# The order of the loads of k and q, and of the casts of V, k and q, in a fused attention + SwiGLU kernel

## The chip, the cores and the metric

The kernel runs on one core of a Trainium2 chip. The metric is the device time of one execution in microseconds (us). "Span" is the time from the first to the last instruction in a profile, some 1.7 to 2.2 us less than the device time.

The engines: TensorE (PE in the profile, PEld its weight loads), VectorE (DVE), ScalarE (ACT), GpSimd (POOL), and SyncE (SP), which only issues DMA here.

## The reference

Causal attention with an additive bias made from a running sum of `s`, then a SwiGLU feed-forward on the result. Batch 8, 8 heads, 576 positions, head size 64; 4608 tokens, model 512, feed-forward 1536.

```python
scores = scale * np.matmul(q, k.transpose(0, 1, 3, 2))
cum = np.cumsum(np.maximum(s, 0.0), axis=-1)
bias = -(cum[:, :, :, None] - cum[:, :, None, :])
scores = np.where(causal, -1e9, scores + np.minimum(bias, 0.0))
attn = softmax(scores)                       # shortened
x = np.matmul(attn, v)                       # then to [4608, 512]
g = x @ w_gate
out = (g / (1 + exp(-g)) * (x @ w_val)) @ w_out
```

## The kernel before

Heads are counted through all batches, 0 to 63. A **half-batch** is four heads; it is the unit in which k and q are loaded (576 KB each), cast to bf16, transposed and used. V is loaded by batch (8 heads), in five chunks. "k 5" below means k of half-batch 5, "V 1" means V of batch 1.

Batch 0's attention runs alone. After that the attention of batch b+1 is woven into nine feed-forward stages of 512 tokens each, of which the first begins at about 30 us. All loads of k, q and V go through one queue, SyncE's, in program order. GpSimd does most of the casts, the causal masks, and issues weights and stores. A **mask** here is the step that blanks the scores of later positions; attention x V of a head cannot start before it.

```python
raw = ctx.enter_context(tc.tile_pool(name="raw", bufs=3))   # k, q as loaded: three half-batches
# ... V as loaded has one buffer (bufs=1): V b+1 waits until V b is cast
NPE = 5          # half-batches 0 to 4 are transposed on TensorE, later ones by DMA

def load_qk(hb):                       # on SyncE's queue
    load_one(hb, "k")
    load_one(hb, "q")

def prep_one(hb, i):                   # a quarter of a half-batch: transpose, copy to KQ
    g, nm = divmod(i, 2)
    nm = ("k", "q")[nm]
    pe_transpose(hb, nm, g)
    for r in range(2):
        pe_out(hb, nm, g, r, nc.scalar if nm == "k" else nc.vector)

PREP_AT = {      # at half-batch h, after (head in it, piece of its scores): which quarter of h + 1
    2: {(1, 3): 0, (2, 1): 1, (2, 3): 2, (3, 1): 3},
    3: {(0, 3): 0, (1, 3): 1, (2, 1): 2, (2, 3): 3},
}

def side(h, step):
    bh = HB * h + step
    if bh == H + 3:                                  # head 11: casts of V 1
        for c in range(5):
            cast_v(1, c, nc.gpsimd)
    if h >= 3 and h + 3 < NHB and step == 0:         # head 12: k, q 6, and so on
        load_qk(h + 3)
    # ... DMA transposes, casts, loads and casts of later V

def attn_items():
    for kk in range(H, BH + 2):
        h, step = divmod(kk, HB)
        if kk < BH:
            if step == 3 and h + 2 < NPE:            # head 11: casts of half-batch 4
                cast_one(h + 2, "k", nc.gpsimd)
                cast_one(h + 2, "q", nc.gpsimd)
            for ci in range(4):
                score_piece(kk, ci)
                if ci == 1:
                    side(h, step)
                # ... then prep_one where PREP_AT says so
        # ... attention x V of earlier heads

# in first_batch(), after the scores of head h:
                if h == 3:
                    aug(2, SP4)                      # bias rows, small DMAs
                    load_qk(3)
                if h == 7:
                    aug(3, SP4)
                    load_v(1, range(5))
                    load_qk(4)
                    cast_one(2, "k", nc.gpsimd)
                    cast_one(2, "q", nc.gpsimd)
                    w_load("o", 0)
                    w_load("o", 1)

hook = {         # after the n-th step of the first feed-forward stage
    # ... 1 to 4: the quarters of half-batch 2
    9: [lambda: cast_one(3, "k", nc.gpsimd), lambda: cast_one(3, "q", nc.gpsimd)],
    21: [lambda: load_qk(5)],
}
```

In the feed-forward, line 571 is the gate matmul, 586 the value matmul, 599 the output matmul. Line 367 is the scores, 405 attention x V, 291 the transposes of k and q, 388 and 383 the masks, 249 the casts of k and q, 176 those of V, 320 the copies of transposed q.

The softmax here doesn't subtract the row's maximum and nothing guards it: scores larger than these inputs give would overflow.

## Time and profile before

| | before |
|---|---|
| device time | 401.94 us median of 3 (400.12 to 403.02) |
| span of the profiled run | 401.8 us (device time 403.55) |
| TensorE busy | 373.3 us (93%) |
| first feed-forward stage | 32.07 to 94.70 us: 62.63 us |
| second, third stage | 42.79 and 40.25 us |

Stage lengths are from the first gate matmul of a stage to that of the next. The view of busy time by window has, for each stretch, its length, busy time (and instructions) of PE, PEld, DVE, ACT and POOL, the granted TensorE clock, the DMA engines' busy share and GB/s. The kernel before:

```profile
52.00:60.00 8.00, 5.45 (x27) 2.54 (x27) 4.75 (x8) 3.27 (x9) 2.96 (x4) 0.79 0.62 180
...
73.90:81.00 7.10, 0.43 (x13) 0.30 (x10) 0.76 (x3) 0.00 (x0) 2.60 (x5) 0.86 0.52 196
81.00:94.70 13.70, 13.38 (x110) 7.66 (x113) 2.87 (x8) 7.09 (x15) 10.72 (x19) 0.83 0.96 220
94.70:137.70 43.00, 42.46 (x373) 24.23 (x380) 30.35 (x57) 26.45 (x55) 27.50 (x46) 1.00 0.73 189
```

TensorE is busy only 5.45 of 8 us in 52 to 60, and in 73.9 to 81 us every engine is idle most of the time; and where TensorE works again its clock is low for some us. Such a stretch in which TensorE has nothing to do is called a **hole** below. The last line is the stage after (and 0.2 us of the next), for comparison: 42.46 of 43.00 us busy, clock 1.00.

### The profile page before, as it was taken

The page shows a single profiled execution, that of the slowest core. Times are in us where ns is not written, and L with a number is a line of the kernel's source. Part 1 is how long each engine was busy: PE and PEld are TensorE (multiplying, and loading weights), DVE is VectorE, ACT ScalarE, POOL GpSimd, SP SyncE. Part 2 cuts the span into 40 slices and gives each one's busy share as a digit, 9 for nine tenths or more (in the row PEclk, how much of TensorE's full clock was granted, in tenths as well). Part 3 has the DMA queues.
Part 4 walks back from the last instruction along what each step waited for, and adds up shares of the span by engine and source line. Part 5 has one row for each costly group of instructions (what it writes and reads, how often), then busy time and mean ns, then how long its engine had stood idle before and what let it go on. Part 6 is the DMA issues. An engine that isn't in the chain of part 4 may idle for free.

```text
span 401.8 us, 7873 instructions
## 1 busy us (share of the span) xinstructions
PE 373.3 (93%) x2943; PEld 207.3 (52%) x2994; DVE 241.5 (60%) x431; ACT 214.3 (53%) x411; POOL 192.4 (48%) x329
## 2 busy tenths in 40 slices
PE   4789979399999999999999999999999999999996
PEld 3575535255555555555555555555555554444442
DVE  7766756315885578627962795479627743842850
ACT  8576954245765665556555655565556522323321
POOL 7581436176578675667565756575542211001001
PEclk9999989979999999999999999999999999999999
DMA  7999975689685998899389939793531114002002
GB/s 248 223 268 207 197 185 125 234 213 244 153 185 148 278 288 176 204 286 232 106 197 277 232 112 190 217 208 104 97 127 27 23 25 135 2 22 82 2 0 105
DMA packets 100534, 64.18 MB, mean 160 GB/s; under 512 B 81888, under 2 KB 85824, under 8 KB 100496
## 3 DMA queue, kind: packets, MB, share of 16 engines
q1 hardware_dynamic: 90672, 45.23, 47.2%
q0 software_dynamic: 9680, 18.32, 17.1%
q8 instruction: 23, 0.38, 0.4%
q14 instruction: 15, 0.12, 0.1%
q10 hardware_dynamic: 144, 0.13, 0.1%
HBM read 37.90 MB, written 19.86 MB: 144 GB/s over the span
## 4 chain that ended last, share of the span: by engine, by line
PE 72%; DMA 9%; SPq 8%; issue 4%; DVE 2%; POOL 2%; ACT 2%; POOLq 0%; DVEq 0%; ACTq 0%
PE bank L599 20%; PE bank L571 18%; PE bank L586 18%; PE bank L367 8%; SPq L169 7%; PE bank L405 5%; DMA rawq<-in_q_dram 3%; DMA rawk<-in_k_dram 2%; DMA pk<-ks 2%; PE wide L367 2%; ACT pt L380 1%; SPq L152 1%; POOL vt L176 1%; DMA XT<-xs 1%; DMA kq<-HL 1%
## 5 line engine op out<-in xcount | busy, mean ns | idle before, releaser
L380 ACT ACTIVATE pt<-bank 128x512 bf16<-128x512 f32 x224 | 104.3, 504 | 52.4 <-PE bank L367 40.2
L578 DVE SCALAR_TENSOR_TENSOR pp<-th,bank 128x512 bf16<-128x512 bf16 x108 | 74.1, 686 | 74.5 <-ACT th L576 73.9
L571 PE MATMUL bank<-XT,wg 128*128 128x512 bf16 x409 | 110.5, 381 | 2.2 <-DMA XT<-xs 0.6
L586 PE MATMUL bank<-XT,wv 128*128 128x512 bf16 x421 | 110.0, 381 | 0.3
L576 ACT ACTIVATE th<-bank 128x512 bf16<-128x512 f32 x108 | 64.5, 597 | 79.3 <-PE bank L571 75.4
L599 PE MATMUL bank<-wo,ht 128*128 128x512 bf16 x415 | 103.5, 383 | 1.0 <-issue 0.2
L591 DVE TENSOR_TENSOR ht<-pp,bank 128x512 bf16<-128x512 bf16 x108 | 74.0, 685 | 9.8 <-PE bank L586 0.9
L367 PE MATMUL bank<-kq 128*128 128x128 bf16 (+4 forms) x504 | 66.7, 242 | 2.4 <-DVE kq L320 2.1
L367 PEld LDWEIGHTS <-kq 128*128 128x128 bf16 x576 | 47.3, 101 | 42.0 <-issue 6.5
L383 POOL TENSOR_SCALAR_AFFINE_SELECT pt<-pt 128x512 bf16<-128x512 bf16 x64 | 41.2, 644 | 43.4 <-ACT pt L380 42.8
L571 PEld LDWEIGHTS <-wg 128*128 128x128 bf16 x432 | 38.5, 98 | 36.9 <-issue 1.8
L599 PEld LDWEIGHTS <-ht 128*128 128x128 bf16 x432 | 38.7, 99 | 36.4 <-issue 1.1
L586 PEld LDWEIGHTS <-wv 128*128 128x128 bf16 x432 | 38.5, 98 | 35.5 <-issue 1.6
L405 PEld LDWEIGHTS <-pt 128*128 128x128 bf16 x960 | 41.8, 98 | 28.9 <-POOL pt L388 6.8
L405 PE MATMUL bank<-vt,pt 128*128 128x65 bf16 x840 | 43.3, 194 | 8.3 <-POOL pt L388 6.7
L439 POOL DMA_DIRECT2D xs<-ot x24 | 21.8, 910 | 58.9 <-DVE ot L422 58.9
L622 POOL DMA_DIRECT2D out_dram<-ysb x35 | 19.6, 562 | 60.9 <-ACT ysb L616 60.9
L616 ACT ACTIVATE ysb<-bank 128x512 f32<-128x512 f32 x35 | 20.9, 598 | 41.5 <-PE bank L599 38.5
L421 DVE RECIPROCAL rc<-bank 128x5 f32<-128x5 f32 x56 | 10.6, 190 | 40.0 <-PE bank L405 39.9
L190 POOL DMA_DIRECT2D kq<-HL x52 | 31.2, 602 | 2.3 <-PE bank L571 1.6
L422 DVE TENSOR_TENSOR ot<-bank,rc 128x320 bf16<-128x320 f32 x56 | 27.5, 492 | 1.9
L249 POOL CAST ck<-rawk 128x1152 bf16<-128x1152 f32 x14 | 16.1, 1148 | 19.3 <-DMA rawk<-in_k_dram 19.3
(66 smaller groups left out, 209.5 us busy)
## 6 DMA issues: line engine op xcount, KB each, us to landing
out_dram<-ysb POOLq DMA_DIRECT2D x35, 256.0 KB, 3.2
rawk<-in_k_dram SPq DMA_DIRECT2D x15, 576.0 KB, 4.8
rawq<-in_q_dram SPq DMA_DIRECT2D x15, 576.0 KB, 6.2
rawv<-in_v_dram SPq DMA_DIRECT2D x32, 256.0 KB, 4.6
xs<-ot POOLq DMA_DIRECT2D x24, 160.0 KB, 3.8
ks<-ck SPq DMA_DIRECT2D x11, 288.0 KB
qs<-cq SPq DMA_DIRECT2D x11, 288.0 KB, 3.9
wg<-in_moe_w_gate_dram POOLq DMA_DIRECT2D x2, 768.0 KB, 12.6
```

Source lines behind the costliest of these rows:

```text
L169: nc.sync.dma_start(t[0:n, c, :, :], v[b, :, c * 128 : c * 128 + n, :].rearrange("h p d -> p h d"),)
L190: engs[hh].dma_start(KQ[hb % 2][r][r0 : r0 + 4, :, e * S : (e + 1) * S], HL[bh : bh + 1, :, :, :],)
L367: nc.tensor.matmul(sc[:, o : o + w], T[:, 1, e * S + 128 * tj : e * S + 128 * (tj + 1)], T[:, 0, e * S + lo : e * S + hi], start=True, sto ...
L380: nc.scalar.activation(pt[:, c0 : c0 + W], sc[:, 0:W], AF.Exp, scale=0.125)
L383: nc.gpsimd.affine_select(pt[:, 1088:1600], pt[:, 1088:1600], pattern=[[0, 4], [1, 128]], compare_op=ALU.is_ge, fill=zreg, base=0, channel ...
L405: nc.tensor.matmul(av[:, bi * (D + 1) : (bi + 1) * (D + 1)], pt[:, c0 : c0 + 128], VT[b % 2][:, tj, h, :], start=(tj == 0), stop=(tj == bi),)
L571: nc.tensor.matmul(pg, WG[j][:, c, f0 : f0 + 128], xt[:, c, :], start=(c == 0), stop=(c == 3),)
L576: nc.scalar.activation(th, pg, AF.Tanh, scale=0.5)
L578: nc.vector.scalar_tensor_tensor(pp, in0=th, scalar=1.0, in1=pg, op0=ALU.add, op1=ALU.mult)
L586: nc.tensor.matmul(pv, WV[j][:, c, f0 : f0 + 128], xt[:, c, :], start=(c == 0), stop=(c == 3),)
L591: nc.vector.tensor_mul(ht, pp, pv)
L599: nc.tensor.matmul(py, hts[ft][:, ts_ * 128 : (ts_ + 1) * 128], WO[ft // WKO][:, ft % WKO, :], start=(ft == 0), stop=(ft == NFT - 1),)
```

## The change

The intent: the loads that are wanted first come first in SyncE's queue, and GpSimd does not stand at a cast whose data is still on its way while V 1 or masks are waiting behind it. `PREP_AT` also moves: half-batch 3 is prepared one head earlier, half-batch 4 one head later. No instruction is added or taken away.

```diff
         PREP_AT = {
-            2: {(1, 3): 0, (2, 1): 1, (2, 3): 2, (3, 1): 3},
-            3: {(0, 3): 0, (1, 3): 1, (2, 1): 2, (2, 3): 3},
+            2: {(0, 3): 0, (1, 3): 1, (2, 1): 2, (2, 3): 3},
+            3: {(1, 3): 0, (2, 1): 1, (2, 3): 2, (3, 1): 3},
         }
@@
-                    if step == 3 and h + 2 < NPE:
-                        cast_one(h + 2, "k", nc.gpsimd)
-                        cast_one(h + 2, "q", nc.gpsimd)
+                    if step == 1 and 3 < h + 1 < NPE:
+                        cast_one(h + 1, "k", nc.gpsimd)
+                        cast_one(h + 1, "q", nc.gpsimd)
@@
                 if h == 3:
                     aug(2, SP4)
-                    load_qk(3)
                 if h == 7:
                     aug(3, SP4)
+                    load_qk(3)
                     load_v(1, range(5))
                     load_qk(4)
                     cast_one(2, "k", nc.gpsimd)
                     cast_one(2, "q", nc.gpsimd)
+                    load_qk(5)
                     w_load("o", 0)
                     w_load("o", 1)
@@
-            9: [lambda: cast_one(3, "k", nc.gpsimd), lambda: cast_one(3, "q", nc.gpsimd)],
-            21: [lambda: load_qk(5)],
+            6: [lambda: cast_one(3, "k", nc.gpsimd), lambda: cast_one(3, "q", nc.gpsimd)],
```

## The prediction

> **What bounds the kernel now.** I read the page first, its 40 slices above all. Each slice is 10.05 us, a digit is tenths busy.
>
> ```profile
> PE   4789979399999999999999999999999999999996
> ...
> PEclk9999989979999999999999999999999999999999
> ```
>
> From slice 9 to slice 38 TensorE is full, so the kernel is TensorE-bound from about 90 us on. The holes are in slice 5 (50 to 60 us), slice 7 (70 to 80 us) and the low clock in slices 5 and 8. That is the first feed-forward stage, interleaved with the attention of batch 1. Its length comes from the windows: it runs from about 30 to 94.7 us.
>
> The view of TensorE in order of time shows the two holes, with what ended them:
>
> ```profile
> 54.21 0.38 PE L367 MATMUL bank<-kq 128*128 128x128 bf16 x4 [2.11 <-DVE kq L320]
> ...
> 80.90 0.35 PE L405 MATMUL bank<-vt,pt 128*128 128x65 bf16 x3 [6.67 <-POOL pt L388]
> ```
>
> The first: scores of head 12 (half-batch 3) wait for the last copy of its transposed q. The second: head 13's attention x V waits for a mask on GpSimd. GpSimd in order of time says why that mask was late:
>
> ```profile
> 56.78 1.15 POOL L249 CAST ck<-rawk 128x1152 bf16<-128x1152 f32 x1 [7.56 <-DMA rawk<-in_k_dram]
> 58.18 1.15 POOL L249 CAST cq<-rawq 128x1152 bf16<-128x1152 f32 x1 [0.26 <-DMA rawq<-in_q_dram]
> ...
> 59.86 2.83 POOL L176 CAST vt<-rawv 128x512 bf16<-128x512 f32 x5
> ...
> 78.40 1.14 POOL L249 CAST ck<-rawk 128x1152 bf16<-128x1152 f32 x1 [11.76 <-DMA rawk<-in_k_dram]
> ```
>
> GpSimd stands 7.56 us at the cast of k 4 and 11.76 us at that of k 5, with V 1's casts and masks behind them. SyncE's queue in order of time shows the reason for the second:
>
> ```profile
> 52.34 0.47 SPq L152 DMA_DIRECT2D rawq<-in_q_dram  x1
> 62.72 5.58 SPq L169 DMA_DIRECT2D rawv<-in_v_dram  x5
> 68.35 0.62 SPq L152 DMA_DIRECT2D rawk<-in_k_dram  x1
> ```
>
> V 2 may be loaded only when V 1's casts end (62.69 us), and k 5 is behind V 2 in one queue, although its buffer was free at 30 us. In between (58 to 62.7 us) the windows give DMA share 0.00. The loop: k 4 delays V 1's casts, these V 2, V 2 delays k 5, and k 5 the masks.
>
> **What the Trainium skill says.**
> - DMA: Bandwidth & Descriptors, "Queues, rings and completion order": each DMA engine takes turns between queue rows, packet by packet. The trace agrees: from 32 to 50 us, while weights load, the two queues moved almost the same number of packets.
>
> ```profile
> q0 software_dynamic: 2412, 2.92, 92.1%
> q1 hardware_dynamic: 2411, 0.62, 26.0%
> ```
>
> - The same page, "Specifications": at least 512 B for line rate. V comes in 256 B packets, k and q in 2304 B. Alone, V 2 moved about 250 GB/s (64.5 to 66 us), k 5 and those after it 383 GB/s (72 to 76 us). Agrees.
> - Perfetto Trace Analysis, "Tensor Engine Instruction (MATMUL, LD_WEIGHTS)": ScalarE, VectorE and GpSimd are strict FIFO. Agrees: masks whose data was there stood behind a cast.
> - TensorE: Matmul & The Clock Gate, "What's actually happening": half clock after an idle window of about 3.4 us, full again after a busy one. Agrees roughly: granted clock 0.50 and 0.54 from 80 to 86 us. It was also low (0.68, 0.76) after the hole of only 2.11 us.
>
> **The change part by part.** No instruction is added or removed; the counts per engine are equal. The order of instructions shows:
>
> 1. k, q 3 leave SyncE's place before the bias rows of half-batch 3 and go behind them: issue at 20.07 becomes about 26.9 us. Weights use those 7 us alone (22 to 24 us: they filled 102% of 16 engines) and then share with k, q 3. From 24 to 30 us each queue got 458 packets, 76 per us; k, q 3 are 512 packets, so they land by 26.9 + 512/76 = 33.6, say 35 us. Their casts (now behind those of half-batch 2, GpSimd free at 31.6 us) end by about 36.5 us. GpSimd had nothing to do until 40.6 us, so this is hidden. Cost 0.
> 2. V 1 begins about 4 us later within the weights. There it goes at 2411/18 = 134 packets per us, alone at 250 GB/s / 256 B = 980 per us. The engines are saturated from 20 to 54 us either way, so the sum of work is unchanged; V 1 loses 4 x 134 = 536 packets of slow time and makes them up in about 0.6 us. It landed by about 55 us (estimate from the queue's packets), now by about 55.7. Cost up to 0.7 us where TensorE needs it.
> 3. Preparation of half-batch 3 comes one head earlier. The hole of 2.11 us goes, and the cold clock behind it: (1-0.68) x 2.79 + (1-0.76) x 2.56 busy us = 1.5 us. Head 12 starts near 52.1.
> 4. The casts of half-batch 4 move behind V 1's. V 1's casts can follow their chunks and end near 56.4, not 62.7 us; TensorE reaches the first attention x V of batch 1 at about 52.1 + 3.4 (its matmuls at full clock) = 55.5 instead of 60.5. The three short waits for V (0.91 + 0.34 + 0.31) vanish but for some tenths. Casts of k, q 4 run at about 59.8 to 62.1 (landed by 59); TensorE wants k 4 at about 61. Near zero.
> 5. k, q 5 are issued behind k, q 4: 1.18 MB at 383 GB/s = 3.1 us, in the idle 58 to 62.7 us, landed by about 62.2. GpSimd gets there at about 63. The 11.76 us wait and TensorE's 6.67 us hole go. V 2 follows at 57 to 67 us; its first two chunks are wanted at about 64, which is about when they land; the mask behind them at 65 is wanted at about 69.
> 6. With the hole the cold clock of 81 to 86 us goes: the window 81 to 94.7 has 13.38 us busy at mean clock 0.83, 13.38 x 0.17 = 2.3 us.
>
> Sum: 2.1 + 1.5 + 1.3 (idle of 60 to 73.9 us: 13.90 - 12.62) + 6.7 + 2.3 = 13.9 us on TensorE's path. I keep 0.6 for the idle that any such stage keeps (the next one: 43.00 us, 42.46 busy) and 0.7 for new small waits: ScalarE gets its half-batch-3 copies earlier, in 40 to 47 us, where it is nearly full (9.15 of 10 us from 40 to 50), and V 1's last chunk. **Gain 12.6 us.** After the stage TensorE is full, so the gain should reach the end: 401.9 - 12.6 = 389.3.
>
> **The rivals.**
> - A wait takes the place: half-batch 4 is now prepared as late as 3 was, and head 16 could wait for its copies as head 12 did (2.1 us and 1.5 of clock). Against: heads 12 to 15 have the batch's attention x V between, 2 to 3 us more TensorE work than stood before head 12. It would make 392.
> - V 1 is starved: if the weights do not gain what k, q 3 leave, V 1 ends some 4 us later, and first attention x V and V 2 with it. For: equal packets per queue. Against: the saturated engines. It would make 393 to 394.
> - The gain is given back after 95 us, because DMA (share 0.73 to 0.97 there) binds a TensorE that runs ahead: k 6 and the transposed k, q 5 must also be earlier. Against: they too leave the queue earlier, as V 2 and k 6 no longer wait until 62.7 and 68 us. It would make 395 to 398.
> - Slower: nothing in the trace speaks for it except k 3 arriving after 41 us, which would take a backlog of 6 us that I do not see.
>
> **Range and chances.** 389.3, with 386 if the new waits are nil and the stage packs better, 395 if a rival takes half. 2% is 401.94/1.02 = 394.1. Faster 0.86, same 0.12, slower 0.02.
>
> **What would show it.** In the changed trace: no TensorE hole over 2 us between 30 and 85 us and clock 1.00 there; GpSimd's waits for k gone or under 3 us; k 5 issued before 58 us, V 2 after it; V 1's casts ending by 57 us; the first stage ending near 82 instead of 94.7 us, and all later stages of the same length (43 and 40.3 us). Wrong if a hole opens at head 16, if V 1's casts come after 59 us, or if the second stage grows by what the first saved.

## The result, and the profile after

389.43 us median of 4 (388.81 to 390.38), against 402.15 us of the kernel before, with a fourth run (400.12 to 403.02). The ratio is 0.9693, with a 95% interval of 0.965 to 0.9735. A ratio is the mean time of one kernel's fast runs over that of the other's fast runs of the same rounds, so it is not quite the ratio of the medians. The change is faster by 3.1%; the prediction said 389.3.

The page of the kernel after, 40 slices of 9.7 us:

```profile
PE   3789999999999999999999999999999999999995
...
PEclk9999999999999999999999999999999999999999
```

The holes over 0.5 us and the low clock are gone. TensorE in order of time has one wait over 0.25 us between 31 and 90 us, where the transposes of k 4 come 0.41 us before their cast:

```profile
60.30 0.45 PE L291 MATMUL bank<-ident,ck 128*128 128x128 bf16 x5 [0.41 <-POOL ck L249]
```

GpSimd in order of time: first the casts of k, q 3, then V 1's, then k, q 4's and k 5's.

```profile
34.68 1.15 POOL L249 CAST ck<-rawk 128x1152 bf16<-128x1152 f32 x1 [4.50 <-DMA rawk<-in_k_dram]
38.13 1.15 POOL L249 CAST cq<-rawq 128x1152 bf16<-128x1152 f32 x1 [2.30 <-PE bank L367]
...
54.62 1.17 POOL L176 CAST vt<-rawv 128x512 bf16<-128x512 f32 x2 [0.86 <-DMA rawv<-in_v_dram]
...
59.10 1.14 POOL L249 CAST ck<-rawk 128x1152 bf16<-128x1152 f32 x1
...
61.87 1.13 POOL L249 CAST ck<-rawk 128x1152 bf16<-128x1152 f32 x1
```

V 1's casts end at 55.8 us, where they ended at 62.7; casts of k, q 4 and k 5 do not wait. The waits at k, q 3 are new (4.50 and 2.30 us; the second is put down to TensorE here, but to q's load in a2_after_again), but the exponentials whose results are masked began only at 38.40 us, so no mask was ready before 39 us, and the second cast ends at 39.28: they cost GpSimd's masks 0.3 us at most. SyncE's queue:

```profile
52.17 0.62 SPq L152 DMA_DIRECT2D rawk<-in_k_dram  x1
52.84 0.47 SPq L152 DMA_DIRECT2D rawq<-in_q_dram  x1
53.40 0.41 SPq L152 DMA_DIRECT2D rawk<-in_k_dram  x1
53.91 0.68 SPq L152 DMA_DIRECT2D rawq<-in_q_dram  x1
55.82 8.39 SPq L169 DMA_DIRECT2D rawv<-in_v_dram  x5
```

k 5 is issued at 53.40, with V 2 behind it. The windows of the kernel after, columns as before:

```profile
52.00:60.00 8.00, 7.84 (x70) 4.26 (x69) 5.71 (x11) 5.80 (x13) 6.60 (x12) 1.00 0.96 323
60.00:73.90 13.90, 13.44 (x163) 9.01 (x167) 8.77 (x19) 8.32 (x17) 9.79 (x17) 1.00 1.00 277
```

TensorE is busy 7.84 of 8 us where it was busy 5.45, at full clock, and the DMA engines work through what was a pause. The first stage takes 48.66 us instead of 62.63, which is 13.97 us less; the second takes 43.04 instead of 42.79, the third 40.24 instead of 40.25.

### The profile page after: what moved, and what is told of

It is laid out like the page before. It is cut to its first block, busy times and chain, and to the rows that moved or that the text cites. A ratio compares the mean times of both kernels' runs of the same rounds, so it can differ in the third digit from the quotient of the medians.

```text
span 387.1 us, 7878 instructions
## 1 busy us (share of the span) xinstructions
PE 367.7 (95%) x2944; PEld 204.5 (53%) x2994; DVE 241.1 (62%) x431; ACT 214.6 (55%) x411; POOL 193.2 (50%) x329
## 4 chain that ended last, share of the span: by engine, by line
PE 83%; DVE 7%; issue 4%; DMA 2%; ACT 2%; POOL 1%; DVEq 0%; SPq 0%; ACTq 0%; POOLq 0%
PE bank L571 22%; PE bank L599 21%; PE bank L586 21%; PE bank L367 9%; PE bank L405 6%; PE wide L367 2%; DVE pp L578 2%; ACT pt L380 1%; DVE ht L591 1%; DVE kq L320 1%; DMA XT<-xs 1%; PE one L405 1%; DMA kq<-HL 1%; DMA xs<-ot 1%; ACT th L576 0%
## 5 line engine op out<-in xcount | busy, mean ns | idle before, releaser
L367 PEld LDWEIGHTS <-kq 128*128 128x128 bf16 x576 | 46.5, 99 | 39.1 <-issue 5.5
L367 PE MATMUL bank<-kq 128*128 128x128 bf16 (+4 forms) x504 | 65.9, 240 | 0.4 <-DVE ht L591 0.2
L616 ACT ACTIVATE ysb<-bank 128x512 f32<-128x512 f32 x35 | 20.9, 597 | 40.9 <-PE bank L599 36.5
L405 PE MATMUL bank<-vt,pt 128*128 128x65 bf16 x840 | 42.8, 194 | 0.0
L388 POOL TENSOR_SCALAR_AFFINE_SELECT pt<-pt 128x64 bf16<-128x64 bf16 x64 | 17.0, 266 | 21.1 <-ACT pt L380 20.9
```

The lines of the kernel that those rows point to most:

```text
L367: nc.tensor.matmul(sc[:, o : o + w], T[:, 1, e * S + 128 * tj : e * S + 128 * (tj + 1)], T[:, 0, e * S + lo : e * S + hi], start=True, sto ...
L405: nc.tensor.matmul(av[:, bi * (D + 1) : (bi + 1) * (D + 1)], pt[:, c0 : c0 + 128], VT[b % 2][:, tj, h, :], start=(tj == 0), stop=(tj == bi),)
```

## The experiments

To compare profiles I use the length of the first stage, because its start lay between 29.35 and 33.02 us over the 14 profiles. The kernel before and the change gave 32.07 and 30.66 us. Until about 17 us all these kernels run the same instructions (the warm-start one excepted), and the profiles already differ there, by when TensorE's matmuls become fast and when the first q arrives. That part of a span's difference (14.7 us in the first pair) is chance. The length of the stage is not wholly free of it: a stage that starts later waits less for the same loads (b2_before_again below), so a difference of 1 or 2 us between two stage lengths says little.

| run | time us (median) | ratio to before | first stage us | third stage us |
|---|---|---|---|---|
| before | 402.15 | | 62.63 | 40.25 |
| before, again | 400.96 (one) | | 59.07 | 40.25 |
| change | 389.43 | 0.9693 | 48.66 | 40.24 |
| change, again | 389.49 | 0.9704 | 48.10 | 42.16 |
| before + k 5 in front of V 2 | 397.86 | 0.9896 | 56.48 | 40.25 |
| before + k 5 in front of k 6 only | 397.59 | 0.9914 | 55.93 | 40.25 |
| change, k 5 at its old place | 396.31 | 0.9865 | 57.01 | 41.41 |
| change, k 5 between V 2 and k 6 | 390.14 | 0.9716 | 50.62 | 40.85 |
| change, casts of 4 in front of V 1's | 396.34 | 0.9867 | 56.86 | 40.24 |
| change, half-batch 3 prepared late | 390.32 | 0.9725 | 49.47 | 41.23 |
| change, k 3 loaded early | 390.54 | 0.9727 | 48.97 | 40.26 |
| change, V 1 in front of k 3 | 405.18 (one) | | 66.01 | 40.25 |
| change, warm start | 392.02 | 0.9764 | 48.14 | 42.64 |
| change, transposes first | 389.92 | 0.97 | 48.08 | 40.26 |

All gave correct results.

### One part alone: k 5 in front of V 2 (e1_only_k5_front)

```diff
                     cast_one(2, "q", nc.gpsimd)
+                    load_qk(5)
@@
-            21: [lambda: load_qk(5)],
```

> The kernel before with one part of the change alone: k, q 5 loaded right behind k, q 4, in front of V 2. Theory (the two holes have separate causes; the 6.67 us hole and the cold clock behind it come from k 5's place in the load queue alone): the hole at head 13 goes, with about 2.3 us of cold clock, so about 393.2 us (402.15 - 9.0); the 2.1 us hole at head 12 and the late casts of V 1 (to about 62.7 us) stay. Rival (V 1's late casts are the root, since V 2's casts also stand in front of the mask): the hole only shrinks, 397 to 400 us.

Measured 397.86 us: 3.9 us under the kernel before in its rounds (401.76), not 9. In time the rival was right. The profile says that the hole at head 13 is gone all the same, as the theory had it. TensorE in order of time:

```profile
33.59 1.04 PE L586 MATMUL bank<-XT,wv 128*128 128x512 bf16 x4 [1.56 <-DMA wv<-in_moe_w_val_dram]
54.27 0.38 PE L367 MATMUL bank<-kq 128*128 128x128 bf16 x4 [2.12 <-DMA rawv<-in_v_dram]
60.85 0.22 PE L405 MATMUL bank<-vt,pt 128*128 128x65 bf16 x2 [1.17 <-POOL vt L176]
```

So neither story was whole. The first line is a wait that the kernel before's profile doesn't have: the first value weights arrived at 33.5 us, and this run's stage had started 1.3 us earlier. A fast start is lost again there. The second line is the hole at head 12, still there; scores read no V, so the releaser named is not the real one (V 1 lands at about the same time), and the last copy of q, at its place as before, is. And the clock was low twice here, 0.50 also from 62.1 to 65.5 us, behind the waits for V 1, where the first profile of the kernel before had 1.00: an estimated 1.7 us (half of 3.4) of the gain went there.

### All parts but that one (e2_k5_back)

```diff
                     cast_one(2, "q", nc.gpsimd)
-                    load_qk(5)
@@
             6: [lambda: cast_one(3, "k", nc.gpsimd), lambda: cast_one(3, "q", nc.gpsimd)],
+            21: [lambda: load_qk(5)],
```

> The changed kernel with k, q 5 back at their old place, which is behind V 2 and also behind k, q 6. Theory: V 1's casts end at about 55.8 us, V 2 is issued then and has landed at about 62, k, q 6 follow, and k 5 lands at about 66.6 to 67.5; GpSimd waits 4 to 6 us for it, the mask of head 13 comes at about 69 and TensorE wants it at 67.9: a hole of 1 to 2 us and some cold clock, so about 392 us. Rival (with V 1's casts early, k 5's place no longer matters): 389.4 us. Rival (k 5's place is worth the same 9 us here as in the kernel before): 398 us.

Measured 396.31 us, 6.9 over the change: 392 was a miss. GpSimd's cast of k 5:

```profile
70.67 1.14 POOL L249 CAST ck<-rawk 128x1152 bf16<-128x1152 f32 x1 [8.69 <-DMA rawk<-in_k_dram]
```

and TensorE's wait for the mask of head 13, which stands behind it:

```profile
73.17 0.35 PE L405 MATMUL bank<-vt,pt 128*128 128x65 bf16 x3 [5.05 <-POOL pt L388]
```

The mechanism was as expected; the landing of k 5 was put 3 to 4 us too early. After the hole the granted clock was 0.50 from 73.2 to 77 us. k 5 alone brings 3.9 us, all but k 5 brings 5.5 (401.76 - 396.31), and both together bring 12.7: **the parts don't add**. (The intervals of these three gains are each 1.4 to 1.7 us wide to either side, so the missing 3.3 us are not sharp; the stage lengths say the same.) Late casts of V 1 and late k 5 each make a first stage of 56 to 57 us alone, and 59 to 63 together. I read this as one delay running while the other does: a TensorE that was held up by V 1 comes later to the mask of head 13 and waits less for it.

### Casts of half-batch 4 back in front of V 1's (e3_cast4_first)

```diff
-                    if step == 1 and 3 < h + 1 < NPE:
-                        cast_one(h + 1, "k", nc.gpsimd)
-                        cast_one(h + 1, "q", nc.gpsimd)
+                    if step == 3 and h + 2 < NPE:
+                        cast_one(h + 2, "k", nc.gpsimd)
+                        cast_one(h + 2, "q", nc.gpsimd)
```

> The changed kernel with the casts of half-batch 4 back in front of V 1's on GpSimd. Theory: k 4 has landed at 56.5, q 4 at 57.9 us, so V 1's casts run from about 59.7 to 62.5; attention x V of head 8, which runs at 54.7 now, waits until about 60.3: a hole of 5 us and about 2 us of cold clock, so about 396 us. Rival (TensorE would find other work in the meantime, or the rest of the stage takes it up): under 392 us.

Measured 396.34 us, as expected; the hole was 6.29 us, not 5. TensorE:

```profile
59.82 0.27 PE L405 MATMUL bank<-vt,pt 128*128 128x65 bf16 x2 [6.29 <-POOL vt L176]
```

This order on GpSimd alone is worth 6.9 us in the changed kernel. V 1, which the change has cast by 55.8 us, stands here behind two casts that can begin only at 56.08 and 57.48 us.

### Half-batch 3 prepared one head later (e4_prep3_late)

```diff
-            2: {(0, 3): 0, (1, 3): 1, (2, 1): 2, (2, 3): 3},
+            2: {(1, 3): 0, (2, 1): 1, (2, 3): 2, (3, 1): 3},
```

> The changed kernel with half-batch 3 prepared one head later, as before. Theory: head 12 again waits about 2.1 us for its last copies, with up to 1.5 us of cold clock behind it, and nothing takes it up: about 392.5 us. Rival (the hole came from copies that VectorE did late for another reason, and is gone without this part): 389.4 us.

Measured 390.32 us, 0.9 over the change, where 3.1 were expected; with ratios of 0.9725 (0.9678 to 0.9771) and 0.9693 the two are not told apart. The hole is there:

```profile
52.43 0.38 PE L367 MATMUL bank<-kq 128*128 128x128 bf16 x4 [2.11 <-DVE kq L320]
```

But the first stage is only 0.81 us longer than the change's. Two things are missing from the bill: the clock stayed at 1.00 (window 52 to 60 us; the last section has why, as far as the traces tell), and the change itself has small waits: three of 0.20 to 0.21 us for VectorE between 39 and 49 us, where this kernel has one of 0.26, and the 0.41 us before the transposes of k 4, which this kernel lacks.

### k, q 3 loaded early again (e5_k3_early)

```diff
                 if h == 3:
                     aug(2, SP4)
+                    load_qk(3)
                 if h == 7:
                     aug(3, SP4)
-                    load_qk(3)
```

> The changed kernel with the loads of k, q 3 back in front of the bias rows of half-batch 3 (issue at about 20 us, not 25.5). The prediction called this move free. New theory, from the run e1_only_k5_front: early k, q 3 share the DMA engines with the first weights; the first val weights land at about 33.4 instead of 30.8 us, and where the first stage starts at 30.7 us TensorE waits about 1.5 us for them; the casts of V 1 end 0 to 0.7 us earlier, which is worth nothing; so about 390.9 us. Rival (the prediction's: free): 389.4 us.

Measured 390.54 us. The wait is there:

```profile
33.98 1.04 PE L586 MATMUL bank<-XT,wv 128*128 128x512 bf16 x4 [1.03 <-DMA wv<-in_moe_w_val_dram]
```

So the move of k, q 3, which the prediction called free, is worth a wait of about 1 us where the start is fast: 1.56 us with a start at 30.73 us (e1_only_k5_front), 1.03 here with 31.65, 0.66 with 31.80 (e6_k5_before_k6), and none over 0.25 us with 32.07 and 33.01 (the kernel before). In the kernel before, the value weights landed at 33.3 us, after the change at 30.8. The medians (390.5 against 389.4 and 389.5, not in the same rounds) agree, but their intervals (0.9701 to 0.9754 and 0.965 to 0.9735) overlap, so the size is not shown.

### What held k 5: V 2 or k, q 6? (e6_k5_before_k6, e8_k5_behind_v2)

The loop of the prediction has "V 2 delays k 5". When I looked for the issue of k 5 in the order of calls, I found k, q 6 in front of it as well: the 21st step of the stage comes after head 12, where k, q 6 are loaded. In the chain of waits of the kernel before, the cast of k 5 is released by the k issued at 69.52 us, the second behind V 2, not by the one of 68.35:

```profile
69.52 8.75 DMA rawk<-in_k_dram
78.40 1.14 POOL ck L249
```

e6_k5_before_k6 is the kernel before with

```diff
-            21: [lambda: load_qk(5)],
+            19: [lambda: load_qk(5)],
```

> The kernel before with k, q 5 still behind V 2, but in front of k, q 6 (the kernel before had them behind both, which the prediction overlooked). Theory: k 5 lands when k 6 did, at about 73.8 instead of 78.3 us; the hole at head 13 shrinks from 6.7 to about 2.2 us, so about 397.5 us, near that of e1_only_k5_front (397.9), and V 2's place matters little. Rival (V 2 is what held k 5 up): 400 us or more.

Measured 397.59 us, as good as e1_only_k5_front (397.86), though k 5 is still behind V 2. GpSimd:

```profile
73.79 1.14 POOL L249 CAST ck<-rawk 128x1152 bf16<-128x1152 f32 x1 [7.10 <-DMA rawk<-in_k_dram]
```

It lands at 73.8 us, and 0.74 us are left of the hole at head 13. e8_k5_behind_v2 is the change with k, q 5 between V 2 and k, q 6:

```diff
-                    load_qk(5)
@@
+            19: [lambda: load_qk(5)],
```

> The changed kernel with k, q 5 behind V 2, but in front of k, q 6. Theory: from the issue of V 2 to the landing of the k behind it the kernel before took 73.8 - 62.7 = 11.1 us; V 2 is issued at 55.9 here, so k 5 lands at about 67, the mask of head 13 comes at about 69.6 and TensorE wants it at about 68: a hole of 1.5 to 2 us, perhaps some cold clock, so about 391.5 us, between 389.4 (change) and 396.3 (e2_k5_back). Rival (V 2 alone is the obstacle, k 6 is not): 395 to 396 us.

Measured 390.14 us: 0.7 over the change and 6.2 under e2_k5_back. The hole at head 13 is 1.12 us long, and the clock stays full. So of the 6.9 us that k 5's place is worth in the changed kernel, k, q 6 account for about 6.2 by the medians. The 0.7 left for V 2 are not told apart from nothing (ratios 0.9716 and 0.9693, with overlapping intervals); the first stage, 50.62 us, is 2.0 to 2.5 us longer than the change's, but it also had an early start.

### The kernel before once more (b2_before_again)

No edit.

> The kernel before, unchanged, for a second profile of it. Expected: the same two holes (2.1 us at head 12, 6 to 7 us at head 13); the start of the first stage at 30.7 or at 32.1 us by the chance of when TensorE's clock turns full near 14 us; where it is 30.7, a wait of about 1.5 us for the first val weights, so that the sum is the same, 400 to 403 us.

Measured 400.96 us. The holes are 2.12 and 4.76 us (6.67 in the first profile). The stage started at 33.01 us, later than expected, and took 59.07 us. So the size of the second hole varies between runs by 2 us: GpSimd waits until the loads land at 76 to 78 us, and a later start of TensorE waits less. The two stages differ by 3.56 us: 1.9 of it is this hole, 0.9 a wait for V 1 that is missing here, and an estimated 0.7 the clock, at half for 4.9 us after the hole in the first profile and for 3.4 in this.

### V 1 in front of k, q 3 (e7_v1_first)

```diff
-                    load_qk(3)
                     load_v(1, range(5))
+                    load_qk(3)
```

> The changed kernel with V 1 in front of k, q 3. Theory (equal packets for the two queues, first in first out within one): V 1's 4608 packets of 256 B go one for one with the weights' packets until these end near 50 us, so V 1 lands near 52 and k 3 only near 53.5 us; TensorE wants the cast of k 3 at 39 us, so a hole of 14 to 16 us opens there, and the time is about 405 us (403 to 408), slower than both kernels. Rival (the queue has room for k 3 beside V 1): under 393 us.

Measured 405.18 us in one run; no run of the kernel before took over 403.59. From 32 to 48 us the two queues moved (packets, MB, share of the 16 engines):

```profile
q0 software_dynamic: 2206, 2.53, 90.5%
q1 hardware_dynamic: 2558, 0.65, 28.9%
```

and TensorE had one hole:

```profile
55.02 0.71 PE L291 MATMUL bank<-ident,ck 128*128 128x128 bf16 x5 [16.40 <-POOL ck L249]
```

V's 256 B packets go about one for one with the weights' packets, and k 3 behind them in the same queue lands at 53.8 us. So the order of k 3 and V 1 matters most of all here, though both kernels had it right.

### A warm start (e9_warm_start), beside the change again (a2_after_again)

```diff
+        keep_warm(26)                    # matmuls of the identity, nobody reads them
         for nm in ("k", "q"):
             for g in range(2):
                 pe_transpose_half(0, nm, g, 0)
@@
                 pe_out(0, nm, g, 1, eng)
+        keep_warm(6)
```

> The changed kernel, unchanged, as the reference for the next run on the same chip, and a second profile of it. Expected 389.4 us; the first stage starts between 29.3 and 30.8 us by chance of the clock and is 48.7 us long; no hole over 0.6 us from 31 to 85 us.

> The changed kernel with 26 matmuls of the identity in front of the first transposes and 6 in front of the first scores, into a PSUM bank that nobody reads, in time that TensorE idles. Theory: the start of the first stage (29.4 to 33.0 us over ten profiles, before any instruction of the change runs) hangs on when TensorE's clock turns full; with it full earlier the stage starts near 29 us, so 1 to 1.5 us less than a2_after_again, about 388.2 us. Rival (ScalarE's exponentials or the bias rows' DMA set the start, not the clock): the same as a2_after_again within 0.4 us.

The change again: 389.49 us; its stage started at 32.57 us, later than I expected. The warm start: 392.02 us, 2.5 us slower, so the edit failed. But it did not do what it was for, and so did not test the theory: the 26 matmuls took 2.95 us, and the transposes behind them still 1.17 us for nine, as without them; the first fast scores were at 13.89 us. The six in front of the scores took 0.82 us on the path. Its start, 31.09 us, lies among the others. For the theory speak the other 13 profiles: put in the order in which the scores become fast for good (4 matmuls at 217 ns each instead of 311; from 10.42 us in e3_cast4_first to 19.33 us in e10_transposes_first), their first stages start in the same order, from 29.35 to 33.02 us. That is an order in profiles, not an experiment.

Both profiles show something else: third stages of 42.16 and 42.64 us, where the kernel before has 40.25 in both its profiles. VectorE in a2_after_again:

```profile
141.15 0.92 DVE L278 COPY kq<-pk 64x1152 bf16<-64x1152 bf16 x2 [1.97 <-DMA pk<-ks]
```

VectorE stands there for transposed k, and the feed-forward's work behind it comes late to TensorE. This wait was 0.62 and 0.83 us in the two profiles of the kernel before and 0.77 in the first of the change (stages 40.24 to 40.25); 1.50 us in e8_k5_behind_v2 (40.85), 1.97 here (42.16) and 3.29 in e9_warm_start (42.64). This is not all of it: TensorE itself waits 0.70 us at 125.19 us for XT, its input that a DMA transposes, and e4_prep3_late, whose VectorE waited 0.94 us, has the same wait (0.53 us) and a third stage of 41.23. So a part of the gain is given back in some runs, 1.9 us in this one and 2.4 in the warm start. That it is because TensorE is now earlier and the transfers aren't is my reading; the next run tests only the loads in front.

### DMA transposes in front of the later loads (e10_transposes_first)

```diff
-            if h >= 3 and h + 3 < NHB and step == 0:
-                load_qk(h + 3)
             if h + 1 < NHB and h + 1 >= NPE:
                 if step == 0:
                     transposes(h + 1)
                     # ...
+            if h >= 3 and h + 3 < NHB and step == 0:
+                load_qk(h + 3)
```

> The changed kernel with the DMA transposes of each later half-batch in front of the loads of k, q two half-batches on, in SyncE's queue. Theory: the third stage is 40.25 us, but 40.9 to 42.6 us in the profiles where VectorE waited 1.5 us or more for the transposed k (a2_after_again: 1.97 us, stage 42.16), because TensorE now runs ahead of the transfers; 1.2 MB of k, q out of the way bring the transposed k about 3 us earlier, so that wait goes, the third stage is 40.25 us, and the median is 388.5 to 389.2 us, a little under 389.5. Rival (the transposes are late for another reason, their scratch written late): wait and stage unchanged, 389.5 us. Miss: over 391 us, if the later loads then come late.

In the profile the waits of VectorE for transposed k are all gone, and the third stage is 40.26 us. The median is 389.92 us, with a ratio of 0.97 (0.967 to 0.9731), no better than the change's 0.9693 and 0.9704. So VectorE's wait is explained by the loads in front, but what its removal is worth over runs is under what these rounds tell apart. No run here beats the change clearly.

Two parts of the change were not undone alone: half-batch 4 prepared one head later, and the casts of k, q 3 three steps earlier.

## Why the prediction was right

The time (389.3 against 389.43 and 389.49) and the sum (13.9 us on the path of TensorE, 13.97 in the first pair of profiles) were right, and so was the bound: TensorE is full from about 31 us on. That the sum fits so well is partly luck: the second pair of profiles gives 59.07 - 48.10 = 10.97 us, and the profile that the sum was read from was of one of the longest executions of its kernel (403.55 us). The sum itself did not need the right shares: it counts the idle and slow time of TensorE in the stage, and the change took nearly all of it away. The shares of the steps were wrong in both directions. By its steps:

- **Step 1, k, q 3 moved at no cost**: nearly. k 3 was put at 33.6 to 35 us; its cast began at 34.68. The casts ended at 39.3 us, not 36.5, just when TensorE wanted k 3 (39.26). What the step missed is a small gain: the first weights come 2.5 us earlier, which e5_k3_early and e1_only_k5_front show as a wait of 1.0 to 1.6 us without it.
- **Step 2, V 1 lands at about 55.7**: nearly. V 1's last packet of 256 B ended at 54.2 us before and 54.3 after, so the cost was 0.1 us and not 0.7; the packet count behind it was confirmed by e7_v1_first (405 expected, 405.18 measured).
- **Step 3, 2.1 + 1.5 us for the hole at head 12**: mis-sized. Undone alone it costs 0.8 us of stage (e4_prep3_late), where the clock didn't drop after the hole and the early preparation has small waits of its own.
- **Step 4, V 1's casts early, "the three short waits vanish"**: right in mechanism, far too small in weight. Undone alone it costs 6.9 us (e3_cast4_first). In the kernel before, these casts cost little to the eye, since TensorE came late to them.
- **Step 5, "k 5 is behind V 2 in one queue"**: this is the step that failed. k 5 was behind V 2 and k, q 6, and the latter was most of what mattered (e6_k5_before_k6, e8_k5_behind_v2); the issue at 68.35 us that the prediction shows is k 6's. Nor was its buffer free at 30 us: by the order in which the three buffers are given out, k, q 6 took the one that the prediction meant, and k 5 had that of half-batch 3, whose casts ran from 42.8 to 45 us. The change moves it in front of both, so the predicted time didn't suffer. The 9 us (6.67 + 2.3) given to this step alone were 3.9 us in time when done alone.
- **Step 6, the clock**: right, 1.00 throughout, where 81 to 94.7 us had 0.83.

The rivals: a wait at head 16 did not appear; V 1 was not starved. "Given back after 95 us" is true in small, with 0 and 1.9 us in the third stage of the change's two profiles, not 6 to 9. Of the signs promised, two were wrong: GpSimd's waits for k were to be gone or under 3 us, and the one at k 3 was 4.50 us, without cost; and all later stages were to keep their length, which the third did in only one of the two profiles.

## What to carry to other kernels

Where one in-order queue feeds one in-order engine, list both orders with the time at which each item is needed and at which it can land, from the calls themselves and not from the trace alone: two loads of the same name look alike there. Undo each part in the final kernel as well as adding it to the first one; when two delays run at the same time, each alone looks small when removed from the first kernel and large when put back into the last. And compare stages, not spans, where the start of a kernel varies by chance.

## What the Trainium skill lacked or had wrong

- TensorE: Matmul & The Clock Gate, "What's actually happening", has the clock fall to half after an idle window of about 3.4 us, and says that the window runs free; it doesn't say how much of a window must be idle. Here it was at half from 55.06 to 58.47 us after a hole of 2.11 us in the kernel before, and stayed at 1.00 after a hole of the same 2.11 us in e4_prep3_late. Worked out from the 14 traces: the spells of half clock inside a run last 3.41 us or a whole multiple (6.83, 17.07), and in each run their edges lie on one grid of 3.41 us. Of the cells of this grid at full clock, all 18 with 2.03 us or more without a matmul were followed by half clock, and none of some 1500 with 1.78 us or less; of four in between, one was. The hole of the kernel before lies in one cell (51.64 to 55.06 us, 2.11 us idle); that of e4_prep3_late is cut by an edge (1.13 us idle in 48.04 to 51.45, 0.99 in the next). So by these traces a hole much shorter than the window is enough if it falls into one cell, and where the cells fall differs from run to run. The ends of matmuls are modelled, so the limit is rough.
- DMA: Bandwidth & Descriptors, "Queues, rings and completion order", has the round robin by packet, which held: 2412 and 2411 packets in 18 us. It lacks what follows for bytes: the queue with 256 B packets got 0.62 MB, the one with the weights 2.92 MB, in the same time (a packet of the profile is one row here, 256 B for V; the page's is typically 9 to 17 descriptors, and whether the two are one unit isn't shown). So a load in small rows is starved while weights load, and everything behind it in its queue too (e7_v1_first: 16.40 us).
